# A fused attention and two-MLP kernel: tiles on the right at multiples of 64 bytes, and a later modelled landing of every transfer

## The chip, the cores and the metric

The kernel runs on one core of one Trainium2 chip. The time is device microseconds of one execution. The engines are TensorE (PE, with its weight loads shown apart as PEld), VectorE (DVE), ScalarE (ACT), GpSimd (POOL) and SyncE (SP), which issues nearly all DMA transfers.

## The reference

Causal attention with a decay, in 4 batches of 8 heads with 576 positions of 64 numbers, followed by two MLPs with squared ReLU on the 2304 tokens (512 to 2048 to 512 each), all in float32:

```python
scores = scale * np.matmul(q, k.transpose(0, 1, 3, 2))
cum = np.cumsum(np.log(np.clip(f, 0.0001, 1.0)), axis=-1)
scores = np.where(causal, -1000000000.0, scores + cum[..., :, None] - cum[..., None, :])
attn = np.exp(scores - np.max(scores, axis=-1, keepdims=True))
attn = attn / (np.sum(attn, axis=-1, keepdims=True) + 1e-09)
x = np.matmul(attn, v)              # to (tokens, heads * 64)
...
h = np.maximum(x @ w_in, 0.0)       # twice, with two pairs of weights
x = h * h @ w_out
```

## The kernel before

**What is computed where.** Every float32 product is made of three products of a high and a low part, so nearly every operand is split by one cast (ACT) and one subtraction (DVE or POOL). The first 64 queries of all heads are done first; queries 64 to 191 go in "pairs" of heads (scores L569, transposes L595, products with v L609 and L611), queries 192 to 575 in 32 "units", one for each head: scores L696 into two PSUM banks `bk`, row maxima L400 on DVE, exponentials on ACT, a transpose by DMA (L714), products with v at L736. A unit's operands come by L635 (`raw`), L638 (`qk<-aug_d`, the rows of the decay) and L680 (`vv`).

**First MLP.** It runs in 9 groups of 256 tokens over 16 blocks of 128 hidden numbers. A block is 12 matmuls at L845 (`hp<-xk,w`), and, a pair of blocks at a time, relu on ACT (L854), the square on DVE (L857, `sq`), the high part on ACT (L867) and the low part on POOL (L870, `gt`), then 12 matmuls at L920 (`yp<-gt,w`). A group's result leaves by L934 or L936 and the store L941 to `y_d`. PE does these blocks between the pairs and units while attention lasts, and alone from about 490 to 624 us.

**Second MLP.** Its products go by a scheme with seven products of half-size blocks instead of eight: L1212 makes 6 matmuls of 384 columns each, DVE adds the results (L1189), then come the square L1223, its parts L1224 (ACT) and L1225, and L1238 (`bk<-w,g`, 512 columns). PE does nothing else from 635 us to the end.

**Weights.** They lie in memory as 64-bit words and are decoded on DVE in three passes of 128 x 512: the first MLP's at L800, L802 and L804 from tiles `st`, `raw` or `tmp` (loaded at L781, then split at L818 and L822), the second MLP's at L1048, L1050 and L1052 from two tiles called `stage` (loaded at L1040) into `word` (output weights, split at L1065 and L1066 and stored to `wo_d`, reloaded at L1233) or `lw` (input weights, combined at L1081 and split at L1099 and L1101). The second MLP's inputs are loaded at L1123, combined at L1155 and split at L1144 (ACT) and L1146 (DVE or POOL).

**What sets the order.** The kernel function first records each operation with its duration, priority and dependences in a `Plan` (`op`), then `run` plays them through: at each modelled time each free engine takes the ready operation of best priority, and the instruction is written at that moment. Operations that either DVE or POOL can do go to the one that is free first. Each engine then carries out its list strictly in that order on the chip, waiting by semaphores. `LAT` is the modelled time from an operation's end to the moment at which others can use its result. For a transfer, `run` has, with `a` = 0.47, `z` = 0.65 and `data` in us (1.46 for 512 KB):

```python
at = max(free[e], lanes[issued % 8])
free[e] = at + dur / o.dmas
dge = max(dge, at) + a
dma = max(dma, dge + z) + o.data / o.dmas
end = lanes[issued % 8] = dma + self.LAT["DMA"] + (self.TURNED if o.turn else 0.0)
```

So a modelled landing also holds one of eight lanes and the tile that the transfer uses.

**Tiles on the right.** SBUF is filled from both ends. The pool `mid` (L303: `sq`, `gt`, `xk`) and, in its place later, a pool with `g` and `r` of the second MLP are the ones on the right; all others, among them the weights `w`, `X`, `stage` and `st`, are on the left. No transfer touches a tile on the right. In the build, right-hand tiles begin at 32 modulo 64 bytes, left-hand ones at 0.

Of the kernel before, what the change touches and what calls it, by code (L numbers as in the profile page):

```python
# [7 lines left out]
F32 = mybir.dt.float32  # L8
# [61 lines left out]
class Plan:  # L70

    LAT = {"PE": 0.27, "ACT": 0.18, "DVE": 0.16, "POOL": 0.16, "SP": 0.95, "DMA": 0.95}
    TICK = 3.413
    COPY, TURN, TURNED = (0.55, 0.47, 0.65), (4.1, 0.63, 0.65), 2.1

# [28 lines left out]
    def run(self):  # L106
        import heapq

        engs = [e for e in self.LAT if e != "DMA"]
        free = dict.fromkeys(engs, 0.0)  # L110
# [11 lines left out]
        while todo:  # L122
            again = True
            while again:
                again = False
                for e in engs:
# [59 lines left out]
                    free[e] = t + dur  # L186
                    end = t + dur + self.LAT[e]
                    if o.data is not None:
# [3 lines left out]
                        for _ in range(o.dmas):  # L192
# [3 lines left out]
                            dma = max(dma, dge + z) + o.data / o.dmas  # L196
                            end = lanes[issued % 8] = dma + self.LAT["DMA"] + (self.TURNED if o.turn else 0.0)
                            issued += 1
# [60 lines left out]
def attention_then_two_squared_relu_mlps(  # L259
# [39 lines left out]

    X = base.tile([128, KD, RING], F32, name="X")  # L300
    xf = X.rearrange("p k c -> p (k c)")
    mid_stack = ExitStack()
    mid = mid_stack.enter_context(tc.tile_pool(name="mid", bufs=1, side="right", reuse_waits="tile"))  # L303
    sq = tiles(mid, 2, [128, 512], F32, "sq")
# [1189 lines left out]
```

## Time and profile before

| What | us |
|---|---|
| Median of 3 runs | 1019.46 (1017.75 to 1022.04) |
| The profiled execution | 1017.82, its span 1016.0 |
| PE busy in the span | 981.3 |
| DVE, ACT, POOL busy | 669.3, 463.2, 338.5 |

The profile is one execution; its time lies 1.64 us below the median. Busy time is what an engine's instructions cover; idle time before an instruction is put down to the event that released it. The clock is the granted clock of PE as a share of 2.4 GHz. Matmuls are pipelined: the next block starts before the end that is shown for the last.

### The profile page before, as it was taken

How to read it: one execution, taken by the hardware profiler on the slowest of the kernel's cores; microseconds unless marked ns; L12 is line 12 of the kernel's file. 1: busy time of each engine (PE TensorE's matmuls, PEld its weight loads, DVE VectorE, ACT ScalarE, POOL GpSimd, SP SyncE). 2: the span in 40 equal slices, each digit the busy share in tenths (PEclk: the TensorE clock that was granted, in tenths of full speed). 3: DMA queues.
4: the chain of work that ended last, by engine and by line, in shares of the span. 5: the costliest groups of instructions: out<-in, count | busy, mean ns of one | idle time of the engine just before them, and what ended most of it. 6: DMA issues, size and time to landing. Idle time of an engine off the chain costs nothing.

```text
span 1016.0 us, 17569 instructions
## 1 busy us (share of the span) xinstructions
PE 981.3 (97%) x6683; PEld 879.9 (87%) x6685; DVE 669.3 (66%) x1400; ACT 463.2 (46%) x919; POOL 338.5 (33%) x281
## 2 busy tenths in 40 slices
PE   5899999999999999999999899999999999999997
PEld 3788898888888888888999899888888898898896
DVE  6998657666667766767376569879685435844443
ACT  3766657767767777776332154222232111311111
POOL 2111143443433434343232335324262122522220
PEclk7899999999999999999999899999999999999999
DMA  9775227656656656755456601863424112231223
GB/s 246 233 217 175 86 72 138 140 114 132 144 109 136 145 108 126 149 102 127 103 182 216 224 24 54 276 209 104 145 89 160 63 64 82 83 104 63 72 74 103
DMA packets 175252, 131.92 MB, mean 130 GB/s; under 512 B 135040, under 2 KB 151680, under 8 KB 175040
## 3 DMA queue, kind: packets, MB, share of 16 engines
q1 hardware_dynamic: 175168, 130.81, 48.2%
q8 instruction: 52, 0.85, 0.3%
q14 instruction: 32, 0.26, 0.1%
HBM read 85.07 MB, written 18.42 MB: 102 GB/s over the span
## 4 chain that ended last, share of the span: by engine, by line
PE 69%; DVE 10%; issue 8%; DMA 8%; POOL 3%; ACT 2%; SPq 1%; POOLq 0%; DVEq 0%; ACTq 0%
PE hp L845 14%; PE yp L920 13%; PE hp L1212 12%; PE bk L1238 10%; PE bk L736 7%; PE yp L1238 5%; PE bk L696 4%; DMA stage<-in_w_dram 4%; POOL g L1225 2%; DMA st<-in_w_dram 2%; DVE w L1101 1%; PE bk L609 1%; PE bk L569 1%; DVE tmp L802 1%; DVE lw L1052 1%
## 5 line engine op out<-in xcount | busy, mean ns | idle before, releaser
L920 PE MATMUL yp<-gt,w 128*128 128x256 f32 x1728 | 236.3, 285 | 5.2 <-POOL gt L870 3.9
L845 PE MATMUL hp<-xk,w 128*128 128x256 f32 x1728 | 232.5, 286 | 0.0
L920 PEld LDWEIGHTS yp<-gt,w 128*128 128x128 f32 x1728 | 221.7, 191 | 8.2 <-POOL gt L870 5.1
L845 PEld LDWEIGHTS hp<-xk,w 128*128 128x128 f32 x1728 | 220.6, 192 | 0.5
L870 POOL TENSOR_TENSOR gt<-sq,gt 128x512 fp32r<-128x512 f32 x72 | 97.4, 1352 | 175.0 <-ACT gt L867 158.8
L1238 PE MATMUL bk<-w,g 128*128 128x512 f32 x576 | 149.5, 396 | 0.2 <-POOL g L1225 0.2
L1225 POOL TENSOR_TENSOR g<-r,g 128x768 fp32r<-128x768 f32 x36 | 67.3, 1870 | 216.0 <-ACT g L1224 180.9
L1212 PE MATMUL hp<-w 128*128 128x384 f32 x630 | 124.7, 337 | 1.8 <-DVE r L1189 1.7
L1224 ACT CAST g<-r 128x768 fp32r<-128x768 f32 x48 | 40.1, 836 | 188.9 <-DVE r L1223 188.7
L1238 PEld LDWEIGHTS bk<-w,g 128*128 128x128 f32 x576 | 107.3, 188 | 18.8 <-POOL g L1225 0.6
L1212 PEld LDWEIGHTS hp<-w 128*128 128x128 f32 x630 | 112.2, 188 | 9.5 <-issue 2.0
L408 ACT ACTIVATE pp<-pp,stat 128x448 f32<-128x448 f32 (+1 forms) x128 | 78.4, 613 | 39.0 <-DVE stat L400 27.5
L430 DVE SCALAR_TENSOR_TENSOR ph<-pp,stat,ph 128x320 f16<-128x320 f32 (+2 forms) x96 | 72.2, 756 | 27.8 <-ACT ph L423 26.7
L400 DVE CUSTOM_DVE_ANT_0 pp<-bk,mask 128x448 f32<-128x448 f32 (+1 forms) x128 | 59.4, 473 | 38.9 <-PE bk L696 38.2
L1189 DVE TENSOR_TENSOR r<-hp,st 128x384 f32<-128x384 f32 x64 | 35.6, 556 | 71.6 <-PE hp L1212 71.6
L736 PE MATMUL bk<-pt,vv 64*128 64x64 f16 (+7 forms) x672 | 77.7, 253 | 0.0
L1223 DVE SCALAR_TENSOR_TENSOR r<-r 128x768 f32<-128x768 f32 x48 | 75.4, 1571 | 1.5
L1212 PE MATMUL hp<-w,far 128*128 128x384 f32 x378 | 75.2, 337 | 0.0
L1238 PE MATMUL yp<-w,g 128*128 128x512 f32 x288 | 75.0, 395 | 0.0
L1212 PEld LDWEIGHTS hp<-w,far 128*128 128x128 f32 x378 | 67.7, 188 | 4.8
L736 PEld LDWEIGHTS <-vv 128*128 128x128 bf16 (+3 forms) x672 | 37.0, 101 | 39.0 <-issue 24.9
L439 POOL TENSOR_TENSOR vv<-vv 128x320 f32<-128x320 f32 x64 | 50.5, 789 | 57.3 <-DMA vv<-in_v_dram 52.7
(167 smaller groups left out, 1247.6 us busy)
## 6 DMA issues: line engine op xcount, KB each, us to landing
w<-wo_d SPq DMA_DIRECT2D x48, 512.0 KB
stage<-in_w_dram SPq DMA_DIRECT2D x26, 512.0 KB
st<-in_w_dram SPq DMA_DIRECT2D x20, 512.0 KB
raw<-in_qk_dram SPq DMA_DIRECT2D x32, 288.0 KB
wo_d<-part SPq DMA_DIRECT2D x16, 512.0 KB
vv<-in_v_dram SPq DMA_DIRECT2D x32, 160.0 KB
raw<-in_w_dram SPq DMA_DIRECT2D x6, 512.0 KB
tmp<-in_w_dram SPq DMA_DIRECT2D x6, 512.0 KB
```

The costliest lines, as they stand in the source:

```text
L400: nc.vector.tensor_tensor_reduce(out=x[:rows, c0:c0 + wd], in0=src, in1=msk, scale=-0.125, scalar=3.0e38 if first else nmax[:rows, 5:6], o ...
L408: nc.scalar.activation(out=x, in_=x, func=AF.Exp, scale=-1.0, bias=nmax[:rows, t:t + 1], accum_out=ssum[:rows, t:t + 1])
L430: nc.vector.scalar_tensor_tensor(out=flat[:rows, z:z + wd], in0=x, scalar=r, in1=flat[:rows, 128 * blk:128 * blk + wd], op0=ALU.mult, op1= ...
L439: eng.tensor_tensor(out=vv()[:, :, 1] if i == 0 else x.bitcast(BF16)[:, :, 0::2], in0=x, in1=x.bitcast(BF16)[:, :, 1::2], op=ALU.subtract)
L736: nc.tensor.matmul(dst.rearrange("p (n c) -> p n c", n=rh.shape[1]), lhsT=lt, rhs=rh, start=(i == 0), stop=(i == len(todo) - 1), skip_grou ...
L845: nc.tensor.matmul(ps, lhsT=lt, rhs=rh, start=(k_ == 0 and c == 0), stop=(k_ == KD - 1 and c == 2))
L870: eng.tensor_tensor(out=gt[1]()[:, :c], in0=sq()[:, :c], in1=f32(gt[0]()[:, :c]), op=ALU.subtract)
L920: nc.tensor.matmul(yp[d // 2]()[:, d % 2], lhsT=lt, rhs=rh, start=(i == 0 and c == 0 and d % 2 == 0), stop=(i == NF - 1 and c == 2), skip_ ...
L1212: nc.tensor.matmul(ps()[:, 0:TH], lhsT=lt, rhs=rh, start=(k_ == 0 and c == 0), stop=(k_ == 1 and c == 2))
L1223: o = op("DVE", dvs(TU), lambda r=r: nc.vector.scalar_tensor_tensor(out=r(), in0=r(), scalar=0.0, in1=r(), op0=ALU.max, op1=ALU.mult), e0, ...
L1225: l = either_vp(TU, lambda e, r=r, g=g: e.tensor_tensor(out=g()[:, 1], in0=r(), in1=f32(g()[:, 0]), op=ALU.subtract), e0, [h], [r, g])
L1238: nc.tensor.matmul(bank(ob[c]), lhsT=g()[:, a, c * 128:(c + 1) * 128], rhs=rw()[:, b], start=(p == 0 and x == 0 and z == 0), stop=(p == NP ...
```

## The change

Two edits. The model's time from the end of a transfer's data to its use rises from 0.95 to 1.65 us, for all transfers. And a tile of 128 x 8 float32 (32 bytes for each partition), which nothing uses, is put first on the right, so that all tiles on the right begin 32 bytes lower, at multiples of 64. The code that records the operations, their priorities and their durations is the same. All lines from 301 on move down by two (L857 becomes L859, and so on).

```diff
--- before.py
+++ after.py
@@ -71,7 +71,7 @@
 
 
 
-    LAT = {"PE": 0.27, "ACT": 0.18, "DVE": 0.16, "POOL": 0.16, "SP": 0.95, "DMA": 0.95}
+    LAT = {"PE": 0.27, "ACT": 0.18, "DVE": 0.16, "POOL": 0.16, "SP": 0.95, "DMA": 1.65}
     TICK = 3.413
     COPY, TURN, TURNED = (0.55, 0.47, 0.65), (4.1, 0.63, 0.65), 2.1
 
@@ -299,6 +299,8 @@
 
     X = base.tile([128, KD, RING], F32, name="X")
     xf = X.rearrange("p k c -> p (k c)")
+
+    ctx.enter_context(tc.tile_pool(name="pad", bufs=1, side="right")).tile([128, 8], F32, name="pad")
     mid_stack = ExitStack()
     mid = mid_stack.enter_context(tc.tile_pool(name="mid", bufs=1, side="right", reuse_waits="tile"))
     sq = tiles(mid, 2, [128, 512], F32, "sq")
```

The lists of all engines come out anew. DVE has 1401 rows in place of 1391, POOL 244 in place of 259, ACT 754 in place of 758, SP 317 in place of 315; 8 or 9 operations with two inputs go to DVE in place of POOL (four of L1066, two of L897, three of L1146, one of L1101, less one of L1155). PE does the same blocks and one more filling matmul at its start. Four places matter below.

DVE among the pairs, at about 72 to 78 us of before (`bk_85` and `bk_84` are banks of scores; `st_82`, `st_83` and `raw` hold weights). Before:

```order
L800 TENSOR_SCALAR tmp<-raw 128x512
L400 ISA pp_105,stat<-bk_85,mask_109 128x192
L400 ISA stat 128x1
L802 SCALAR_TENSOR_TENSOR tmp<-raw,tmp 128x512
L800 TENSOR_SCALAR tmp<-st_82 128x512
L804 SCALAR_TENSOR_TENSOR tmp<-raw,tmp 128x512
L400 ISA pp_105,stat<-bk_85,mask_109 128x192
L400 ISA stat 128x1
L400 ISA pp_104,stat<-bk_84,mask_109 128x192
```

Now, for the scores of the same count (names of buffers are four higher):

```order
L804 SCALAR_TENSOR_TENSOR tmp<-st_87,tmp 128x512
L402 ISA pp_109,stat<-bk_89,mask_113 128x192
L402 ISA stat 128x1
L402 ISA pp_109,stat<-bk_89,mask_113 128x192
L402 ISA stat 128x1
L899 TENSOR_TENSOR xk_85<-X,xk_85 128x512
L806 SCALAR_TENSOR_TENSOR tmp<-st_87,tmp 128x512
L802 TENSOR_SCALAR tmp<-raw 128x512
L824 TENSOR_TENSOR w<-tmp,w 128x512
L804 SCALAR_TENSOR_TENSOR tmp<-raw,tmp 128x512
L802 TENSOR_SCALAR tmp<-st_86 128x512
```

The two maxima of one bank had the rest of a weight decode and the first pass of another between them; now they follow one another, and the decode follows them. The next four maxima stand at row 169, behind 18 rows of decode and splits.

DVE near the end of the first MLP, at about 549 to 558 us of before (`lw` are words of the input weights, `stage_5704` and `stage_5705` the two tiles). Before:

```order
L857 SCALAR_TENSOR_TENSOR sq_74<-hp_89,sq_74 128x512
L1048 TENSOR_SCALAR lw_5713<-stage_5704 128x512
L1048 TENSOR_SCALAR lw_5713<-stage_5705 128x512
L1050 SCALAR_TENSOR_TENSOR lw_5713<-stage_5704,lw_5713 128x512
L1050 SCALAR_TENSOR_TENSOR lw_5713<-stage_5705,lw_5713 128x512
L1052 SCALAR_TENSOR_TENSOR lw_5713<-stage_5704,lw_5713 128x512
L857 SCALAR_TENSOR_TENSOR sq_73<-hp_88,sq_73 128x512
L1052 SCALAR_TENSOR_TENSOR lw_5713<-stage_5705,lw_5713 128x512
```

Now:

```order
L1054 SCALAR_TENSOR_TENSOR word_5764<-stage_5762,word_5764 128x512
L1050 TENSOR_SCALAR lw_5770<-stage_5761 128x512
L1052 SCALAR_TENSOR_TENSOR lw_5770<-stage_5761,lw_5770 128x512
L859 SCALAR_TENSOR_TENSOR sq_78<-hp_93,sq_78 128x512
L1054 SCALAR_TENSOR_TENSOR lw_5770<-stage_5761,lw_5770 128x512
L1050 TENSOR_SCALAR lw_5770<-stage_5762 128x512
L1052 SCALAR_TENSOR_TENSOR lw_5770<-stage_5762,lw_5770 128x512
L1054 SCALAR_TENSOR_TENSOR lw_5770<-stage_5762,lw_5770 128x512
L859 SCALAR_TENSOR_TENSOR sq_77<-hp_92,sq_77 128x512
```

The passes of the two words of `lw` went in turns, with both first passes ahead of the square; now one word's first and second pass stand ahead of the square and the other word's after it.

PE among the units, where the first scores of a unit come ahead of the product L736 of the one before (at about 251 to 256 us of before):

```order
L920 MATMUL yp_90<-gt_75,w 128x256
L920 MATMUL yp_90<-gt_76,w 128x256
L920 MATMUL yp_90<-gt_75,w 128x256 x2
L920 MATMUL yp_90<-gt_76,w 128x256
L920 MATMUL yp_90<-gt_75,w 128x256
L845 MATMUL hp_89<-xk_80,w 128x256 x6
L845 MATMUL hp_89<-xk_79,w 128x256 x6
L696 MATMUL bk_84<-qk_1305 128x320
L696 MATMUL bk_84<-qk_1303 128x320
L736 LDWEIGHTS vv_102
L736 MATMUL bk_87<-pt_99,vv_102 128x384
```

Now, at the second such place:

```order
L922 MATMUL yp_94<-gt_81,w 128x256
L922 MATMUL yp_94<-gt_82,w 128x256
L922 MATMUL yp_94<-gt_81,w 128x256 x2
L922 MATMUL yp_94<-gt_82,w 128x256
L922 MATMUL yp_94<-gt_81,w 128x256
L698 MATMUL bk_88<-qk_1299 128x320
L698 MATMUL bk_88<-qk_1297 128x320
L738 LDWEIGHTS vv_106
L738 MATMUL bk_91<-pt_103,vv_106 128x384
```

In both there are two blocks of 12 ahead of the two scores (their first is above the rows shown). There are two such places in the first list after the opening units and two in the second, seven units earlier.

DVE where the second MLP begins, from its first addition (to `st`) to its second (to `r`), at 629 to 635 us of before (`word_5707`, and now `word_5763` and `word_5764`, are words of the output weights). Before:

```order
L1189 TENSOR_TENSOR st_83<-hp_89,st_82 128x384
L1146 TENSOR_TENSOR w<-X,w 128x384 x2
L1050 SCALAR_TENSOR_TENSOR word_5707<-stage_5705,word_5707 128x512
L936 COPY st_83<-yp_91 128x512
L1189 TENSOR_TENSOR r_6993<-hp_88,st_82 128x384
L1189 TENSOR_TENSOR st_82<-hp_89,st_83 128x384
```

Now:

```order
L1191 TENSOR_TENSOR st_87<-hp_93,st_86 128x384
L1148 TENSOR_TENSOR w<-X,w 128x768
L1148 TENSOR_TENSOR w<-X,w 128x384
L1083 TENSOR_TENSOR X<-lw_5771,X 128x256
L1050 TENSOR_SCALAR word_5763<-stage_5761 128x512
L1050 TENSOR_SCALAR word_5764<-stage_5762 128x512
L1148 TENSOR_TENSOR w<-X,w 128x768
L1103 TENSOR_TENSOR w<-X,w 128x4x256
L938 COPY st_87<-yp_94 128x512
L1191 TENSOR_TENSOR r_6993<-hp_92,st_86 128x384
```

Two narrow L1146, one decode pass and the copy L936 stood between the additions; now three L1148, one L1083, two first passes, one L1103 and the copy do.

## Rows read from the trace of the kernel before

**Rows 1.** The page, busy time, share of the span and count.

```profile
PE 981.3 (97%) x6683; PEld 879.9 (87%) x6685; DVE 669.3 (66%) x1400; ACT 463.2 (46%) x919; POOL 338.5 (33%) x281
```

**Rows 2.** Windows: stretch, length, busy PE, PEld, DVE, ACT, POOL, clock, DMA, GB/s.

```profile
60.00:80.00 20.00, 16.47 (x121) 14.44 (x120) 18.50 (x47) 13.57 (x38) 3.74 (x3) 0.97 0.74 218
...
580.00:600.00 20.00, 20.00 (x155) 20.00 (x156) 9.01 (x13) 8.31 (x13) 5.39 (x5) 0.91 0.31 100
...
640.00:660.00 20.00, 20.00 (x101) 18.00 (x100) 17.24 (x27) 4.85 (x8) 7.45 (x6) 1.00 0.84 262
```

**Rows 3.** Lines, PE: line, tiles, shape, count, busy us, mean ns, idle before, releasers.

```profile
L920 PE MATMUL yp<-gt,w 128*128 128x256 f32 x1728 | 236.3, 285 | 5.2 <-POOL gt L870 3.9 <-ACT gt L867 1.4
...
L1212 PE MATMUL hp<-w 128*128 128x384 f32 x630 | 124.7, 337 | 1.8 <-DVE r L1189 1.7
...
L696 PE MATMUL bk<-qk 68*128 68x288 f32 (+5 forms) x256 | 55.4, 334 | 2.9 <-DMA qk<-aug_d 2.8
...
L569 PE MATMUL bk<-qk_a 66*128 66x192 f32 (+2 forms) x96 | 16.9, 320 | 6.5 <-DVE stat L400 3.9 <-DMA qk_a<-aug_d 2.6
```

**Rows 4.** Timeline of PE: start, length, instruction, idle before it and releaser.

```profile
77.39 1.90 PE L569 MATMUL bk<-qk_a 66*128 66x192 f32 x12 [3.27 <-DVE stat L400]
...
579.94 2.08 PE L920 MATMUL yp<-gt,w 128*128 128x256 f32 x11 [1.22 <-POOL gt L870]
581.81 2.63 PE L845 MATMUL hp<-xk,w 128*128 128x256 f32 x12
584.28 1.60 PE L920 MATMUL yp<-gt,w 128*128 128x256 f32 x12
...
635.48 6.72 PE L1212 MATMUL hp<-w 128*128 128x384 f32 x35 [1.69 <-DVE r L1189]
```

**Rows 5.** Timeline of DVE around 75 and 556 us.

```profile
74.96 0.43 DVE L800 TENSOR_SCALAR tmp<-st 128x512 uint32<-128x512 uint32 x1 [1.04 <-DMA st<-in_w_dram]
...
555.06 0.43 DVE L1048 TENSOR_SCALAR lw<-stage 128x512 uint32<-128x512 uint32 x1 [2.64 <-DMA stage<-in_w_dram]
...
557.21 0.68 DVE L857 SCALAR_TENSOR_TENSOR sq<-hp,sq 128x512 f32<-128x512 f32 x1
```

**Rows 6.** Waits of DVE for weight loads: total us, times, longest.

```profile
DVE lw L1048 <- DMA stage<-in_w_dram: 11.3, 7, 2.6
...
DVE word L1048 <- DMA stage<-in_w_dram: 10.8, 8, 2.6
...
DVE tmp L800 <- DMA st<-in_w_dram: 7.5, 5, 4.3
```

**Rows 7.** Chain that ended last, loads in it: start, time to landing.

```profile
69.39 5.55 DMA st<-in_w_dram
...
252.95 2.67 DMA qk<-aug_d
...
548.84 6.20 DMA stage<-in_w_dram
...
562.99 3.67 DMA stage<-in_w_dram
```

**Rows 8.** Timeline of DVE where the second MLP begins.

```profile
627.38 2.05 DVE L1146 TENSOR_TENSOR w<-X,w 128x768 fp32r<-128x768 f32 x1
...
629.82 3.85 DVE L1146 TENSOR_TENSOR w<-X,w 128x384 fp32r<-128x384 f32 x2
...
634.80 0.54 DVE L1189 TENSOR_TENSOR r<-hp,st 128x384 f32<-128x384 f32 x1
```

**Rows 9.** Lines by form: PE and ACT work, aligned and misaligned on the right.

```profile
L845 PE MATMUL hp<-xk,w 128*128 128x256 f32 x1728 | 232.5, 286 | 0.0
...
L696 PE MATMUL bk<-qk 128*128 128x448 f32 x32 | 12.2, 382 | 0.0
...
L867 ACT CAST gt<-sq 128x512 fp32r<-128x512 f32 x72 | 44.5, 619 | 46.3 <-DVE sq L857 45.3
...
L818 ACT CAST w<-tmp 128x512 fp32r<-128x512 f32 x30 | 18.4, 618 | 20.3 <-DVE tmp L804 20.2
```

## The prediction, made before the run

> **What bounds the kernel now.** I read the busy line of the page first: TensorE (PE) is busy 97% of the span, VectorE (DVE) 66%, the rest less [rows 1]. So the time is PE's own work plus what PE loses, and a change of order can only win back losses. The windows view says where they are. From 640 us on PE is busy 20.00 of every 20 us at a granted clock of 1.00; in 60 to 80 us it is busy 16.47 while DVE is busy 18.50 [rows 2]. The lines view tells what ended PE's idle times: L920 lost 5.2 us to the squared hidden tiles, L1212 1.8 to an addition on DVE, L696 2.9 to a load of score rows, L569 3.9 to the row maxima of DVE (its other 2.6 lie before 45 us) [rows 3]. That is 5.2 + 1.8 + 2.9 + 3.9 = 13.8 us behind the first 45 us.
>
> A second loss shows only in the clock. The block of 12 matmuls at 584.28 takes 1.60 us; the ones at 579.94 (11 matmuls, which would take 1.48) and 581.81 take 2.08 and 2.63, 1.6 us too much together, right behind an idle time of 1.22 us [rows 4], and the granted clock of that window is 0.91 although PE is busy in all of it [rows 2]: a stretch at 1.2 GHz instead of 2.4. There are four such stretches (near 80, 125, 562 and 582 us; the windows of the first and the last are shown): 4 x 1.6 = 6.4 us. All that this change can win on PE is thus about 13.8 + 6.4 = 20.2 us, 2% of the time, and only where a modelled landing was too early.
>
> That it was too early is in the timeline of DVE and in its waits. DVE works its list strictly in order. At 555.06 it has stood 2.64 us before the first decode pass of a weight word, and the square L857 starts only at 557.21, behind it [rows 5]; PE waits at L920 for what is made of such squares. DVE waits 11.3 + 10.8 us in 15 waits on the `stage` loads and 7.5 us in 5 on the `st` loads [rows 6]. By the constants of the old model a 512 KB load lands 0.47 + 0.65 + 1.46 + 0.95 = 3.53 us after its issue; those on the chain took 3.67 to 6.20 [rows 7]. With 1.65 the model says 4.23.
>
> **Skill against row.** The trace's shortest of these loads on the chain took 3.67 us [rows 7]. The Trainium skill, "SBUF — State Buffer", section "The DMA setup-cost knee (why "@ 1 MiB" ≠ asymptote)", puts a transfer at about 2 us plus its bytes at 436 GB/s, by which I estimate 3.2 us for 512 KB; by that page the old model was late enough already, and the sum would be 0 instead of -7.4 (rival E). The measured landings disagree with it, and the measurement decides.
>
> **The change part by part.** The first line moves nothing on the chip itself: the list of each engine is written by a planner that believes every transfer later by 0.70 us. Five places:
>
> 1. Up to 45 us the lists stand nearly as before: 0, with 1.5 either way.
>
> 2. Pairs, 45 to 135 us. PE waited 3.27 us before the scores at 77.39 for a maximum [rows 4] that stood on DVE's list behind the decode pass at 74.96, which itself waited 1.04 us for its load [rows 5]. In the new list both maxima of that bank stand next to each other, ahead of those passes (first two orders above). So 3.27 could go whole; but DVE is nearly full here [rows 2], and the next four maxima stand behind some 18 rows of decode, among them a first pass that can wait for its load in the same way, so I leave 1.04 and a little to them and take 2.1, and with it the one stretch at 1.2 GHz that followed it, 1.6: **-3.7**. Bounds: 0, if only the pair that waits is another one, and -3.9 - 2 x 1.6 = -7.1.
>
> 3. Units, 135 to 500 us. Twice in before PE reaches the first scores of the next unit after two blocks of 12 and waits for `qk<-aug_d`, 2.8 us together [rows 3]; that load took 2.67 [rows 7]; the model said 0.47 + 0.65 + 0.05 + 0.95 = 2.12 and now says 2.82. But the new list of PE has the same figure twice again (the order of PE above): two blocks, then two scores, then L738. No other block is put in between, so I take **-0.5**; bounds 0 and -2.8.
>
> 4. Last groups of the first MLP, 505 to 585 us. Before, one square stood behind the first passes of two words, each with its own load (2.64 us idle at the second [rows 5]). In the new list a square stands behind the passes of one word (third and fourth order above). The 15 waits sum to 22.1 us, 1.47 each [rows 6]; 0.70 of each, 48%, becomes other work of DVE in front of it. 48% of L920's 5.2 is 2.5; the two stretches at 1.2 GHz follow idle times of 1.0 to 1.2 us there, and the wait of L696 of the same size elsewhere had none, so I let 1.4 of the two go, 2.2: **-4.7**. Bounds: 0 and -5.2 - 3.2 = -8.4. What is late next is the decode itself: both lists hold 11 word passes between the same two evacuations, so the rate of the words doesn't rise, only the squares stop waiting for them.
>
> 5. Change to the second MLP, 585 to 640 us. Eight or nine two-input operations move from GpSimd (POOL) to DVE. PE waits 1.69 us for the addition L1189 [rows 4]. Before, 634.80 - 629.82 = 5.0 us of DVE lie ahead of it (two narrow L1146, a decode pass, L936) [rows 8]. In the new list eight rows do: L1148 three times, L1083, two first passes L1050, L1103, L938. At the price of an undisturbed row they take about as long, at the price of 627.38 (2.05 for 768 columns) and 629.82 (1.93 each) [rows 8] about 3 more. PE's work ahead of it is the same: 0 to +3, and 1.6 if the clock falls: **+1.5**. Bounds 0 and +4.6.
>
> From 640 us on PE has no loss to win back [rows 2], and the same blocks: 0.
>
> **The shift by 32 bytes.** Right-hand tiles began at 32 modulo 64, now at 0. PE reads `xk` from there at L845: 286 ns for 256 columns, against 337 for 384 at L1212, where all tiles were aligned already [rows 9, 3]. 128 columns are 53 ns at 2.4 GHz, so L845 would be 284 at L1212's price: 2 ns, on 1728 matmuls of L845 and perhaps as many of L920, 7 us at most. Against that, L696 with 448 columns, aligned, takes 382 [rows 9], more per column than either. ScalarE writes a misaligned `gt` in 619 ns and an aligned `w` in 618 [rows 9]. I take **0**; bounds 0 and -7.
>
> **Sum.** 0 - 3.7 - 0.5 - 4.7 + 1.5 + 0 = -7.4 us. The profiled execution took 1017.82, so it would take 1010.4; the median of three, 1.64 above it, 1019.46 - 7.4 = 1012.1. I say **1012**.
>
> **The rivals.** (A) The forecast: waits shrink where a landing was modelled too early.
>
> (B) The waits only move. The two `stage` tiles and the decode set the pace: a load can be issued only when a tile is free, so the same 22.1 us of waits come back behind other rows, and the squares or maxima of another place stand behind them. For it: equal words between two evacuations in both lists, DVE 18.50 of 20 busy at 60 to 80 us. Against it: one word instead of two ahead of a square. Terms 2 and 4 fall to a fifth: -1.7 - 0.5 + 1.5, about 1018.5.
>
> (C) Slower, by DVE where the second MLP begins. All eight rows ahead of the second addition run at the disturbed price (three forms at 2.05, 2.05 and 1.93, the other five about 5, 11 us against 5.0: +6), the two first passes of words each find their load missing by the longest wait of 2.6 (+5.2) [rows 6], and PE's two idle times each bring a stretch at 1.2 GHz (+3.2): +14.4 in place of +1.5, 1025. For it: 3.85 us for two narrow forms in before. Against it: the words' loads there are issued long before. It decides from about 14 us on, where it outweighs terms 2 to 4 (8.9) by over 5.
>
> (D) The alignment counts on PE after all: 7 us more, 1005. The first sign would be L845 below 284 ns.
>
> (E) The landings that cost PE something are those of about 3.6 us, as at 562.99 [rows 7], which the old model had right within 0.14, and those of 5 and 6 us are beyond the new one too. Then 0.70 more moves rows without need: 1019.5, no change. For it: 548.84 with 6.20; against it: the 15 waits, 1.47 us each, come with landings that late. This is what the page named above would make of it.
>
> **How the numbers follow.** A 0.48, B 0.24, E 0.05, C and its like 0.12, D 0.11. 0.5%, about what a measurement of this kernel can tell from no change, is 5.1 us: faster means below 1014.4, slower above 1024.6. A's own range, by its bounds taken half-way, is 1007 to 1017; its slower part, about an eighth, counts as the same. Faster 0.43 + 0.11 = 0.54; same 0.05 + 0.24 + 0.05 = 0.34; slower 0.12. For 8 in 10 the range takes in A, B and most of D: 1004 to 1020.
>
> **What would show it.** Right: DVE's waits on `stage` fall from 22.1 us to about 12; L922 (as L920 is called then) loses 2.5 to 3 us instead of 5.2; L571 loses under 4.5 instead of 6.5; the windows at 560 to 600 us have a clock above 0.95; L1214 loses 2 to 4 us; L845's mean stays at 286. Wrong: `stage` waits of 20 us and a clock of 0.91 in new places (B); L1214 with 8 us or more (C); L847 at 284 or less (D). A long wait in the first 45 us, where I assume none, would break the sum in either direction.

## The result, and the profile after

The changed kernel takes 1008.56 us (median of 4 runs, 1008.09 to 1010.64) against 1018.74 for the kernel before on the same chip: a ratio of 0.989 (95% interval 0.986 to 0.992), some 10 to 11 us. 1012 had been forecast. The sign was right and the number came near; what the gain is made of was not as forecast, as the experiments show.

The busy line of the page of the changed kernel, which answers to [rows 1]:

```profile
span 1008.8 us, 17582 instructions
...
PE 977.4 (97%) x6686; PEld 873.5 (87%) x6686; DVE 671.4 (67%) x1409; ACT 462.6 (46%) x918; POOL 322.2 (32%) x273
```

This profiled execution took 1010.64, the slowest of the four, so it shows 7.2 of the 10 us. PE is busy 3.9 us less, though it does the same blocks, and idle 3.3 us less. The windows view by the five places of the sum tells more. Columns: stretch, its length, busy PE, PEld, DVE, ACT, POOL, granted clock, DMA share, GB/s. The kernel before:

```profile
0.00:45.00 45.00, 30.02 (x249) 22.81 (x251) 37.10 (x92) 22.51 (x58) 9.87 (x30) 0.73 0.92 259
45.00:135.00 90.00, 85.19 (x626) 75.70 (x625) 68.10 (x179) 55.96 (x148) 14.46 (x11) 0.96 0.49 144
135.00:500.00 365.00, 362.06 (x2943) 320.11 (x2942) 246.15 (x708) 261.01 (x529) 144.56 (x143) 1.00 0.60 125
500.00:585.00 85.00, 80.26 (x633) 78.24 (x632) 53.13 (x79) 22.26 (x39) 27.29 (x19) 0.96 0.60 195
585.00:645.00 60.00, 57.96 (x440) 56.56 (x439) 49.34 (x65) 28.47 (x44) 25.47 (x17) 1.00 0.27 83
```

The changed kernel:

```profile
0.00:45.00 45.00, 31.73 (x247) 23.83 (x248) 34.66 (x86) 20.45 (x52) 9.73 (x30) 0.73 0.89 254
45.00:135.00 90.00, 86.85 (x634) 76.22 (x633) 70.78 (x187) 58.06 (x153) 13.50 (x10) 0.96 0.51 147
135.00:500.00 365.00, 358.92 (x2930) 317.06 (x2929) 245.06 (x711) 260.32 (x528) 140.09 (x141) 0.99 0.59 123
500.00:585.00 85.00, 84.18 (x715) 82.73 (x714) 56.55 (x77) 26.07 (x45) 24.95 (x19) 1.00 0.64 200
585.00:645.00 60.00, 57.14 (x408) 54.42 (x407) 55.81 (x81) 24.51 (x38) 22.33 (x15) 1.00 0.36 119
```

Length less busy PE is PE's idle time. It falls by 1.7 us in the first 45 us, by 1.7 among the pairs and by 3.9 in the last groups of the first MLP, where the clock also rises from 0.96 to 1.00. Among the units it rises from 2.9 to 6.1 us, and the clock there falls to 0.99. The change to the second MLP costs 0.8 us more. Together the idle time is 3.3 us less. In the clock nothing is won over the whole: before and now 13.7 us lie at 1.2 GHz between 45 and 990 us, only elsewhere (now 6.8 us among the pairs and 6.8 among the units).

The lines view (line, tiles, shape, count, busy us, mean ns, idle before, releasers), answering to [rows 3] and to the first line of [rows 9], and the waits of DVE that answer to [rows 6]:

```profile
L847 PE MATMUL hp<-xk,w 128*128 128x256 f32 x1728 | 231.5, 284 | 3.1 <-DVE xk L899 1.6 <-DVE w L824 0.8 <-ACT xk L534 0.5
L922 PE MATMUL yp<-gt,w 128*128 128x256 f32 x1728 | 230.4, 282 | 1.3 <-POOL gt L872 1.3
...
L1214 PE MATMUL hp<-w 128*128 128x384 f32 x630 | 125.1, 338 | 2.4 <-DVE r L1191 2.2
...
L698 PE MATMUL bk<-qk 68*128 68x288 f32 (+5 forms) x256 | 55.7, 335 | 4.6 <-DMA qk<-aug_d 3.7 <-DVE stat L402 0.5 <-DVE qk L659 0.4
...
L571 PE MATMUL bk<-qk_a 66*128 66x192 f32 (+2 forms) x96 | 18.3, 343 | 1.6 <-DVE stat L402 1.6
```

```profile
DVE tmp L802 <- DMA st<-in_w_dram: 7.0, 4, 4.7
...
DVE word L1050 <- DMA stage<-in_w_dram: 4.5, 6, 1.3
...
DVE lw L1050 <- DMA stage<-in_w_dram: 3.4, 3, 1.3
```

L922 loses 1.3 us in place of L920's 5.2, and DVE waits 7.9 us for the `stage` loads in place of 22.1: the squares no longer stand behind late words. The waits on the `st` loads of the first MLP hardly change, 7.0 in place of 7.5. But L698 loses 4.6 in place of 2.9, L847 loses 3.1 where it lost nothing, and the means of L847 and L922 are 284 and 282 ns in place of 286 and 285, which the prediction had named as the sign of rival D.

### The profile page after: what moved, and what is told of

Its sections match the earlier page's. It is cut to its first block, busy times and chain, and to the rows that moved or that the text cites. A ratio compares the mean times of both kernels' runs of the same rounds, so it can differ in the third digit from the quotient of the medians.

```text
span 1008.8 us, 17582 instructions
## 1 busy us (share of the span) xinstructions
PE 977.4 (97%) x6686; PEld 873.5 (87%) x6686; DVE 671.4 (67%) x1409; ACT 462.6 (46%) x918; POOL 322.2 (32%) x273
## 4 chain that ended last, share of the span: by engine, by line
PE 73%; DVE 9%; issue 8%; DMA 5%; POOL 3%; ACT 2%; SPq 0%; POOLq 0%; DVEq 0%; ACTq 0%
PE hp L847 16%; PE yp L922 15%; PE hp L1214 13%; PE bk L1240 10%; PE bk L738 7%; PE yp L1240 5%; PE bk L698 4%; POOL g L1227 2%; DMA st<-in_w_dram 2%; DMA stage<-in_w_dram 2%; DVE w L1103 1%; PE bk L571 1%; DVE tmp L804 1%; PE bk L611 1%; DVE X L1083 1%
## 5 line engine op out<-in xcount | busy, mean ns | idle before, releaser
L847 PE MATMUL hp<-xk,w 128*128 128x256 f32 x1728 | 231.5, 284 | 3.1 <-DVE xk L899 1.6
L922 PE MATMUL yp<-gt,w 128*128 128x256 f32 x1728 | 230.4, 282 | 1.3 <-POOL gt L872 1.3
L847 PEld LDWEIGHTS hp<-xk,w 128*128 128x128 f32 x1728 | 218.0, 192 | 5.8 <-DVE xk L899 2.0
L922 PEld LDWEIGHTS yp<-gt,w 128*128 128x128 f32 x1728 | 217.7, 190 | 2.8 <-POOL gt L872 1.9
L1214 PE MATMUL hp<-w 128*128 128x384 f32 x630 | 125.1, 338 | 2.4 <-DVE r L1191 2.2
L1214 PEld LDWEIGHTS hp<-w 128*128 128x128 f32 x630 | 112.6, 188 | 10.7 <-issue 2.4
L432 DVE SCALAR_TENSOR_TENSOR ph<-pp,stat,ph 128x320 f16<-128x320 f32 (+2 forms) x96 | 69.4, 725 | 24.9 <-ACT ph L425 23.6
L1214 PE MATMUL hp<-w,far 128*128 128x384 f32 x378 | 75.3, 337 | 0.0
L1214 PEld LDWEIGHTS hp<-w,far 128*128 128x128 f32 x378 | 67.9, 188 | 5.0
L425 ACT ACTIVATE ph<-pp,stat 128x320 f16<-128x320 f32 (+2 forms) x96 | 63.6, 664 | 14.5 <-DVE stat L419 13.2
```

The source lines that it names most:

```text
L425: nc.scalar.activation(out=a, in_=x, func=AF.Copy, scale=r)
L432: nc.vector.scalar_tensor_tensor(out=flat[:rows, z:z + wd], in0=x, scalar=r, in1=flat[:rows, 128 * blk:128 * blk + wd], op0=ALU.mult, op1= ...
L847: nc.tensor.matmul(ps, lhsT=lt, rhs=rh, start=(k_ == 0 and c == 0), stop=(k_ == KD - 1 and c == 2))
L922: nc.tensor.matmul(yp[d // 2]()[:, d % 2], lhsT=lt, rhs=rh, start=(i == 0 and c == 0 and d % 2 == 0), stop=(i == NF - 1 and c == 2), skip_ ...
L1214: nc.tensor.matmul(ps()[:, 0:TH], lhsT=lt, rhs=rh, start=(k_ == 0 and c == 0), stop=(k_ == 1 and c == 2))
```

## The experiments

Ratios are to the kernel before on the same chip. Pace means the mean time from the start of a line's matmul to the start of PE's next matmul, worked out from the starts in the trace, leaving out gaps of over one and a half times the median; before it is 120.0 ns at L845 and 119.9 at L920.

### One edit at a time

`lat_only` has the later landing and no new tile; its lists are row for row those of the changed kernel:

```diff
-    LAT = {"PE": 0.27, "ACT": 0.18, "DVE": 0.16, "POOL": 0.16, "SP": 0.95, "DMA": 0.95}
+    LAT = {"PE": 0.27, "ACT": 0.18, "DVE": 0.16, "POOL": 0.16, "SP": 0.95, "DMA": 1.65}
```

> The later modelled landing without the unused tile on the right: the lists of all engines are row for row those of the changed kernel, and the right-hand tiles begin at 32 modulo 64 as before. Theory (the order alone): the whole gain, a ratio of 0.989 to the kernel before (-10 to -11 us), L845 at the mean of the changed kernel's L847 (284 ns), and the same idle times of PE at the same places. Rival (alignment): a part of the gain is missing, up to 7 us, a ratio of 0.992 to 0.996, and L845 slower by 2 ns or more.

`pad_only` has the new tile and the old landing time, so the order of before:

```diff
+    ctx.enter_context(tc.tile_pool(name="pad", bufs=1, side="right")).tile([128, 8], F32, name="pad")
```

> The unused tile on the right with the old landing time of 0.95: the order is that of the kernel before, the right-hand tiles are at multiples of 64. Theory (the order alone): no change, a ratio of 1.000 within 0.3%, PE idle about 28 us with the waits of before, L847 at 286 ns. Rival (alignment): up to 7 us faster, a ratio of 0.993 to 0.997.

`after_again` is the changed kernel itself, beside them on the same chip.

> The changed kernel beside the others on the same chip: a ratio of 0.987 to 0.991 to the kernel before by both theories; it is here so that the single edits can be set against it directly.

| Kernel | Runs | Median us | Ratio | 95% interval | Pace of L845, L920 (ns) |
|---|---|---|---|---|---|
| before, same chip | 28 | 1017.35 | 1 | | 120.0, 119.9 |
| later landing alone | 11 | 1013.62 | 0.9955 | 0.993 to 0.998 | 120.0, 120.0 |
| shift by 32 bytes alone | 12 | 1013.60 | 0.9955 | 0.993 to 0.998 | 117.6, 117.5 |
| both (the change, again) | 6 | 1006.94 | 0.9895 | 0.987 to 0.992 | 117.5, 117.5 |

My theory, that the order gives the whole gain, half falls: by the ratios the order alone is worth about 4.6 us, and the shift as much by itself (some 3.7 each by the medians). The shift speeds up PE's own work: 2.4 ns less at each of 3456 matmuls is 8.3 us. Alone, only about half of that reaches the time. The lines view of `pad_only` shows one place where it is lost: PE, now quicker, waits longer for the squares that stand behind late words:

```profile
L922 PE MATMUL yp<-gt,w 128*128 128x256 f32 x1728 | 233.0, 283 | 8.4 <-POOL gt L872 6.7 <-ACT gt L869 1.7
```

8.4 us at this line where [rows 3] has 5.2. With the later landing under it those waits are 1.3, and from the second to the fourth row of the table the shift is worth 1013.62 - 1006.94 = 6.7 us (6.1 by the ratios). The windows of `lat_only` (columns as above), whose order is the changed one at the old pace:

```profile
45.00:135.00 90.00, 88.14 (x672) 78.48 (x673) 70.41 (x186) 60.01 (x155) 17.42 (x14) 1.00 0.53 157
135.00:500.00 365.00, 359.43 (x2874) 316.67 (x2873) 242.05 (x708) 256.48 (x522) 136.09 (x138) 0.98 0.58 120
500.00:585.00 85.00, 85.00 (x711) 83.75 (x710) 57.54 (x77) 25.70 (x44) 25.63 (x19) 1.00 0.62 200
585.00:645.00 60.00, 57.77 (x405) 55.92 (x405) 54.51 (x79) 24.97 (x38) 22.20 (x15) 0.97 0.33 110
```

Here the pairs are idle 1.9 us in place of 4.8 and have no stretch at 1.2 GHz; the last groups are idle not at all; the units lose 5.6 in place of 2.9, with the clock down to 0.98.

### The stage loads alone

`stage_only` gives 1.65 us to the loads of L1040 and 0.95 to all others. In this kernel and in the three of the next section `o.land` is the landing time of one operation; the lines that set it for all the others are left out:

```diff
-                    end = lanes[issued % 8] = dma + self.LAT["DMA"] + (self.TURNED if o.turn else 0.0)
+                    end = lanes[issued % 8] = dma + o.land + (self.TURNED if o.turn else 0.0)
...
         o = op("SP", P.COPY[0], load, prio, deps, [st], data=1.46 if wide else 0.73)
+        o.land = 1.65
```

> The landing time is 1.65 for the loads of the second MLP's weights into the two stage tiles alone (L1040), 0.95 for all other transfers, and there is no unused tile: up to about 500 us the order is that of the kernel before. Theory (squares behind late words): the last groups of the first MLP, 505 to 585 us, lose under 1.5 us of PE instead of 4.7 and no stretch at 1.2 GHz is left there (a gain of 6 to 8 us), the pairs and the units stay as before, so the ratio is 0.993 to 0.995. Rival (the whole order had to move): the gain needs the other transfers too, and the ratio is above 0.997.

1013.76 us, 0.9963 (0.995 to 0.998): 3.8 us, less than the 6 to 8 that I expected, and almost the whole of what the later landing gives. The place itself behaves as expected; the next one takes part of it back. Its windows:

```profile
500.00:585.00 85.00, 84.35 (x702) 82.79 (x701) 57.91 (x80) 25.50 (x44) 27.09 (x20) 1.00 0.61 198
585.00:645.00 60.00, 56.71 (x398) 54.28 (x397) 54.93 (x73) 25.00 (x38) 23.35 (x16) 0.97 0.29 96
```

Idle time in the last groups falls from 4.7 to 0.6 us with no stretch at 1.2 GHz; at the change to the second MLP it rises from 2.0 to 3.3, and 3.4 us at 1.2 GHz stand there now.

### Which transfers should land later

`pad_weights` and `pad_stage` have the new tile on the right and 1.65 us for the weight loads of both MLPs (L781 and L1040), or for the stage loads alone. The edit of `pad_weights` (`pad_stage` has the second added line and the tile alone):

```diff
     def weights(m, i, prio, prio2, deps, free, stage, words):
...
+            o.land = 1.65
...
     def words(i, z, stage, dst, prio, deps, uses):
...
+        o.land = 1.65
...
+    ctx.enter_context(tc.tile_pool(name="pad", bufs=1, side="right")).tile([128, 8], F32, name="pad")
```

`units_old` is the changed kernel with 0.95 for the transfers of the units:

```diff
+    unit_ = unit
+
+    def unit(*a):
+        P.now = 0.95
+        got = unit_(*a)
+        P.now = 1.65
+        return got
```

> Right-hand tiles at multiples of 64 bytes, and 1.65 us of landing for the weight loads alone (L781 and L1040); 0.95 for all other transfers, so that the units of attention keep the order of before. Theory (the later landing helps where weights are decoded and costs PE 2 to 3 us among the units, which lost 5.3 to 6.0 us in place of 2.8): 2 to 3 us below the changed kernel, a ratio of 0.986 to 0.988 to the kernel before; PE loses about 3 us between 135 and 500 us. Rival (the later landing of all transfers is needed, or the times of the places shift into each other): the same as the changed kernel or above, 0.989 to 0.992.

> Right-hand tiles at multiples of 64 bytes, and 1.65 us of landing for the stage loads (L1040) alone. Theory: the alignment's 7 us less what faster blocks give back in waits, and the 3.7 us that the stage loads alone gave without the alignment: a ratio of 0.988 to 0.991, as good as the changed kernel without any change among pairs and units. Rival (the alignment's gain is lost to waits unless the whole order moves): 0.993 or above.

> The changed kernel, but the transfers of the units of attention alone keep the landing time of 0.95. The order of the units on PE is that of the kernel before. Theory (the later landing of those transfers costs PE time at the changes of group and the stretch at 1.2 GHz behind it): PE idle 3 us in place of 6 between 135 and 500 us, no stretch of 6.8 us at 1.2 GHz there, 3 to 5 us below the changed kernel, a ratio of 0.985 to 0.987. Rival (what is won there is lost where the second MLP begins, as with the later landing for the weights alone): the ratio of the changed kernel, 0.989, and over 3 us idle at 585 to 645 us.

0.9894 (0.987 to 0.992), 0.9888 (0.986 to 0.991) and 0.9898 (0.987 to 0.993): none beats the changed kernel, which had 0.9895. `pad_stage` came out as expected, the other two as their rivals had it. `pad_stage` equals the changed kernel with the later landing on the stage loads alone, so no run shows a gain from the later landing of any other transfer. And since its lists are those of `stage_only`, the shift is worth 0.9963 - 0.9888, or 7.6 us, once the stage loads land later in the model: nearly the whole 8.3, though the two intervals leave some 3 us either way.

The units do lose less where their transfers keep the old time: idle 3.6 us in `pad_weights` and 3.8 in `units_old`, in place of 6.1. The windows of `pad_weights`, and then two of `units_old`:

```profile
135.00:500.00 365.00, 361.45 (x2970) 318.42 (x2969) 245.67 (x710) 260.50 (x530) 145.35 (x143) 1.00 0.60 127
```

```profile
135.00:500.00 365.00, 361.23 (x2932) 317.54 (x2932) 241.91 (x704) 257.08 (x525) 140.86 (x139) 0.98 0.60 124
...
585.00:645.00 60.00, 56.22 (x370) 52.82 (x369) 56.10 (x73) 22.24 (x35) 24.50 (x17) 0.97 0.39 135
```

All profiled executions divide in this way: PE is idle 2.9 to 3.8 us among the units in the seven in which these transfers have 0.95, and 5.0 to 6.1 in the seven in which they have 1.65. So the later landing of these transfers is what cost PE 2.3 to 2.5 us there. But that isn't a gain of the whole. In `units_old` the order at the change to the second MLP is another one, and PE's timeline there has

```profile
608.77 1.56 PE L931 MATMUL yp<-gt,w 128*128 128x256 f32 x11 [0.98 <-POOL gt L881]
610.17 1.21 PE L1223 MATMUL hp<-w 128*128 128x384 f32 x6
611.23 1.57 PE L931 MATMUL yp<-gt,w 128*128 128x256 f32 x12
613.36 0.38 PE L931 MATMUL yp<-gt,w 128*128 128x256 f32 x1 [0.57 <-ACT gt L878]
615.58 4.04 PE L931 MATMUL yp<-gt,w 128*128 128x256 f32 x23 [1.83 <-POOL gt L881]
```

The block after the wait of 1.83 us takes 4.04 us for 23 matmuls, which at full pace take 2.9: a stretch at 1.2 GHz. In this stretch, 585 to 645 us, PE is idle 3.8 us in place of 2.9 in the changed kernel. The gain among the units was partly moved, and not kept in the time. A landing time that gives both was not found.

### What in the address counts

`xk_off` puts the unused tile between `gt` and `xk`, so that `sq` and `gt` are at multiples of 64 bytes and `xk` is back at 32 modulo 64:

```diff
-    ctx.enter_context(tc.tile_pool(name="pad", bufs=1, side="right")).tile([128, 8], F32, name="pad")
...
+    mid.tile([128, 8], F32, name="pad")
     XK = Pool(tiles(mid, 3, [128, 2, 2, GA], F32R, "xk"), True)
```

> The changed kernel with its unused tile moved inside the pool between gt and xk: sq and gt stay at multiples of 64 bytes, xk (and later g and r) are back at 32 modulo 64. The order is that of the changed kernel. From one matmul's start to the next, before had 120.0 ns at L845 (moving operand xk) and 119.9 at L920 (moving operand gt), the changed kernel 117.6 at both. Theory (the address of the moving operand sets the pace): L845 back to 120.0 ns, L920 stays at 117.6. Rival (any misaligned tile, or the writes of the other engines into them, slows both): both change, or neither.

Pace: 119.8 ns at its L848 (the moving operand is `xk`), 117.8 at its L923 (`gt`). Its timeline of PE shows it without any working; the starts of the blocks of 12 alternate by 1.45 and 1.41 us:

```profile
540.90 1.60 PE L848 MATMUL hp<-xk,w 128*128 128x256 f32 x12
542.35 1.57 PE L923 MATMUL yp<-gt,w 128*128 128x256 f32 x12
543.76 1.60 PE L848 MATMUL hp<-xk,w 128*128 128x256 f32 x12
545.20 1.57 PE L923 MATMUL yp<-gt,w 128*128 128x256 f32 x12
```

So the pace of a line goes with where its own moving operand lies: the shifted `xk`, which other engines write, leaves L923 at its pace.

`left_off` keeps the right side of the changed kernel and shifts the whole left side by 32 bytes; `right_64` makes the unused tile 64 bytes, so that the right side is at 32 modulo 128 (before 96, in the changed kernel 64):

```diff
+    ctx.enter_context(tc.tile_pool(name="off", bufs=1)).tile([128, 8], F32, name="off")
     wp = ctx.enter_context(tc.tile_pool(name="wp", bufs=16))
```

```diff
-.tile([128, 8], F32, name="pad")
+.tile([128, 16], F32, name="pad")
```

> The order of the changed kernel and aligned tiles on the right, but an unused tile of 32 bytes put first on the left, so that all weights, score operands, inputs of the second MLP and staging tiles lie at 32 modulo 64. Theory (moving operand, a price that goes with the columns): L1212 (384 columns, moving operand on the left) goes from 176.2 to about 179.8 ns, L1238 (512 columns, moving weights on the left) from 233.5 to about 238, L845 and L920 stay at 117.6 though their stationary operands are shifted; some 8 us more PE work. Rival (a fixed price for each matmul): 2.4 ns more at each, 178.6 and 235.9. Second rival (the stationary operand counts too): L845 and L920 go up as well.

> The changed kernel with an unused tile of 64 instead of 32 bytes: the right-hand tiles begin at 32 modulo 128; in the kernel before it was 96 modulo 128, in the changed one 64. The order is that of the changed kernel. Theory (multiples of 64 matter): L845 and L920 go from 117.6 back to 120.0 ns from one start to the next, some 8 us more work of PE. Rival (only 96 modulo 128 was bad; the shift of the left side by 32 had left L1212 and L1238 at their pace): both stay at 117.6.

In both the theory fell. With the left side shifted, L1212 has 176.4 ns (before 175.6, changed 176.2) and L1238 233.2 (233.6 and 233.5), though their moving operands now lie at 32 modulo 64. And `right_64`, with `xk` and `gt` at 32 modulo 64 again, is not slow: 117.2 and 117.4. Its blocks, 1.40 us from start to start:

```profile
541.89 1.56 PE L847 MATMUL hp<-xk,w 128*128 128x256 f32 x12
543.29 1.56 PE L922 MATMUL yp<-gt,w 128*128 128x256 f32 x12
544.69 1.56 PE L847 MATMUL hp<-xk,w 128*128 128x256 f32 x12
```

So "a multiple of 64" is not the rule, though the change moved the tiles to one: 32 modulo 64 was slow at 96 modulo 128 and is not at 32 modulo 128. Two rules fit L845 and L920 in all placements that ran. Either a moving operand at 96 modulo 128 is slow by itself; those of L1212 and L1238 were never there. Or the distance from the stationary operand (`w`) to the moving one counts: it was 96 modulo 128 in before and for `xk` in `xk_off` (119.8 to 120.0 ns), 64 in the changed kernel and 32 in `left_off` and `right_64` (117.2 to 117.6); at L1212, whose operands both lie on the left, it never changed.

Each rule has a line against it. Against the first: in the build of `left_off` both operands of the scores (its L699, L698 in the changed kernel) lie at 96 modulo 128. From a matmul of 288 columns to the next of the same scores it takes 134.5 ns there, and 134.6 and 134.7 in the two kernels below with the same shift; in the eleven profiled executions with both at 64 it takes 134.1 to 139.3. Against the second: L1238, with 512 columns and `g` as its stationary operand, had a distance of 96 in `left_off` and `right_64` and was not slow (233.2 and 233.1 ns, before 233.6). The number of columns may count as well. No run separates these, and the rule stays open.

### The faster-looking versions, timed

`left_off` took 1001.78 us in its one execution. It was timed as `left_off_timed`, and `units_old` with the same shift as `units_old_left`.

> The changed kernel with all left-hand tiles at 32 modulo 64, timed: its one execution took 1001.78 us, where the two profiled executions of the changed kernel took 1010.6 and 1010.8. L845 and L920 stood at 117.2 and 117.3 in place of 117.6 ns, which is 1.2 us, and its pairs lost 5 us less. Theory (the order and the pace are the same; one execution differs by where the stretches at 1.2 GHz fall): 1 to 2 us below the changed kernel, a ratio of 0.986 to 0.990 to the kernel before. Rival (weights at another offset than the moving operand help by themselves): 0.981 to 0.985.

> The last one with the left-hand tiles at 32 modulo 64 as well. Theory: as the last one and 1 to 2 us less, a ratio of 0.983 to 0.986; rival (weights at another offset than the moving operand help by themselves): 0.978 to 0.981.

0.9881 (0.985 to 0.991; 6 runs from 1001.2 to 1010.5) and 0.9888 (0.986 to 0.991; 1002.3 to 1007.8). The first is as the theory of equal pace has it (0.986 to 0.990), the second a little above its range (0.983 to 0.986); the single execution of `left_off` was a lucky one. No version is shown to beat the changed kernel.

## Why the prediction was right, and where it was not

**Bound.** That an order can win back only PE's idle times and the clock held: the pace of `lat_only` is 120.0 ns as before. That the whole change could win back no more did not hold: the second edit changed PE's own work.

**Term 1, to 45 us: 0 with 1.5 either way.** The idle time fell by 1.7 us, just outside.

**Term 2, pairs: -3.7.** The wait of 3.27 us is gone, as argued from the two maxima side by side; idle time fell by 1.7 in the changed kernel and by 2.9 in `lat_only`. The 1.6 of the clock did not come in the changed kernel: a wait of 1.13 us stands before a block there,

```profile
86.21 2.65 PE L571 MATMUL bk<-qk_a 66*128 66x192 f32 x12 [1.13 <-DVE stat L402]
88.51 5.46 PE L922 MATMUL yp<-gt,w 128*128 128x256 f32 x24
```

and 24 matmuls take 5.46 us in place of 3.0. Of the seven profiled executions with these same lists, four have such a stretch among the pairs and three (`lat_only`, `left_off`, `right_64`) have none. Whether it falls there is not settled by the order alone.

**Term 3, units: -0.5.** Wrong in sign: +3.1 us idle, and 6.8 us at 1.2 GHz. I had seen the same figure of blocks in both lists and took the waits to be the same or smaller. At the two places they are 2.04 and 1.63 us, 3.7 together where [rows 3] had 2.8, and I had not followed the list past the figure. Behind the second place DVE comes late with the inputs of the next group:

```profile
326.40 0.42 PE L698 MATMUL bk<-qk 68*128 68x320 f32 x1 [1.63 <-DMA qk<-aug_d]
...
330.42 0.54 PE L698 MATMUL bk<-qk 128*128 128x288 f32 x2 [0.46 <-DVE stat L402]
...
333.58 6.36 PE L847 MATMUL hp<-xk,w 128*128 128x256 f32 x29 [1.46 <-DVE xk L899]
```

29 matmuls take 6.36 us in place of 3.6. `units_old`, in which these transfers alone have their old time back, is idle 2.3 us less there: the cause of the idle time is shown, the whole of the price is not (the clock of `units_old` was 0.98 there too).

**Term 4, last groups: -4.7.** Right in mechanism, too small in size: 3.9 us of idle time and, with two stretches of 3.4 us at 1.2 GHz gone, 3.4 more, 7.3 together. The step that failed was "48% of L920's 5.2": with a square behind one word in place of two, L922 still lost 1.3, so that three quarters went. `stage_only` shows the same from this place alone.

**Term 5, change to the second MLP: +1.5.** +0.8 in idle time, and the wait before the second addition is 2.25 us in place of 1.69. The eight rows on DVE ran at the undisturbed price except for the first two L1148 (2.55 us together).

**The shift: 0, bounds 0 and -7.** The mis-sized term. The bound had the right row, 2 ns by which L845 was dearer than L1212, and nearly the right size. I set it aside because L696, aligned, was dearer still, and because ACT wrote both kinds of tiles alike; but L696 has other lengths, and ACT's writes are not PE's reads. The pace for each column would have told more than the means: before, L845 takes 120.0 / 256 = 0.469 ns, L1212 175.6 / 384 = 0.457 and L1238 233.6 / 512 = 0.456; now L847 takes 0.459. So L845 was the one that was dear, while the 53 ns that the prediction takes for 128 columns are shown by no run (from 256 to 384 columns the pace rises by 58.6 ns in the changed kernel). `xk_off` shows that the pace of L845 hangs on where `xk` lies. Rival D was right as to PE: 8.3 us of work, of which 4.6 (alone) to 6.7 (with the order) reach the time.

**Sum.** Forecast -7.4, all of it from the order. Measured -10 to -11: the order alone gives 0.45% or 4.6 us, since the units and the clock gave back what the last groups won beyond the forecast. That the total came out near is luck in this respect: one term that was set to zero stood in for what another took back. Of the signs named beforehand those of the order came (the `stage` waits fell further than to 12, L922 and L571 lost less than was said, L1214 lost 2.4); the one on L845's mean did not, and pointed to D.

Of the rivals, B's cause did not come: the `stage` waits fell from 22.1 us to 7.9 instead of moving. Idle time did come back at another place, among the units, but from the later landing of other transfers. (By B's own terms its sum is 1018.8, not 1018.5; nothing hangs on it.) C did not come: DVE found the words of those passes loaded. E fell with `stage_only`, where the later landing of those loads alone emptied the place of its waits. By the fit of the Trainium skill's page "SBUF — State Buffer", section "The DMA setup-cost knee (why "@ 1 MiB" ≠ asymptote)", the prediction estimated 3.2 us for a load of 512 KB. The loads of [rows 7] took 3.67 to 6.20, and with 4.23 modelled DVE still waits 7.9 us for such loads, so here the measured landings stand against that estimate.

## What to carry to other kernels

Where lists are written by a planner, a landing time that is too early shows as in-order engines standing before a load with ready work behind; give the later time first to the transfers that show this wait, and follow every list past the place that is mended, since a planner moves the other places too. Two edits in one change need two runs, each alone: a forecast that is right in sum can be wrong in both. And compare the time from start to start of the same block at different placements of its operands: here 2.4 ns on 3456 matmuls is 8.3 us of work, where the order alone gave 4.6.

## What the runs showed of the hardware that I had not expected

- The pace of a matmul of 256 columns in this kernel depends on where its operands start: 119.8 to 120.1 ns with `xk` or `gt` at 96 modulo 128 and the weights at 0, 117.2 to 117.8 with them at 64 or 32. `xk` alone moved L848 alone. Among the other placements no difference is shown: with the left side shifted, and the stationary `w` with it, L845 had 117.2 in place of 117.6, but in `units_old_left` 117.5 in place of 117.4 in `units_old`.
- PE had stood idle shortly before each stretch at 1.2 GHz behind the first 45 us, but idle time of the same size is not followed by one each time: 2.01 us before the scores at 176.8 of `lat_only` is, 2.04 us before those at 183.2 of the changed kernel is not. The later landing alone took 1008.4 us in an execution whose mean granted clock was 0.985 and 1020.5 in one with 0.972; the 12 of the shift alone spread over 8.8 us. So single executions of two kernels can differ by that much without any cause in the kernels.
